# W_out's first 128 rows converted during attention; W_in's conversions at other steps

## Chip, cores, metric

The kernel runs on one core of one Trainium2 chip. The metric is the device time of one execution in microseconds (us). A profiled execution gives the rows below; its span runs from the first to the last instruction.

## What is computed

Soft-capped attention, a soft mixture of experts (MoE) on its output, and a two-matrix feed-forward block on that. W_in and W_out are float64; all else is float32. Cut from the reference:

```python
scores = cap * np.tanh(scale * np.matmul(q, k.transpose(0, 1, 3, 2)) / cap)   # 4 batches, 12 heads, 448 x 448, head_dim 64
attn = softmax(scores); x = np.matmul(attn, v)                                # -> x (1792, 768)
logits = x @ phi                                                              # 32 slots, 8 experts x 4
slot_out[e] = np.maximum(slot_input[e] @ w1[e], 0.0) @ w2[e]                  # w1 (768, 1024), w2 (1024, 768)
x = softmax(logits, 1) @ slot_out
h = x @ w_in                                                                  # w_in (768, 2048) float64
g = np.maximum(h, 0.0) + alpha * np.minimum(h, 0.0)
return (g @ w_out).astype(np.float32)                                         # w_out (2048, 768) float64
```

## The kernel before

**Attention** works on 24 pairs of heads, four steps each, one step for each chunk of 128 keys (the fourth is the tail of 64). Steps are counted by `g`, 0 to 95, and pair `i` has steps 4i to 4i+3. In a step TensorE makes the scores (`s<-qh,kh`, `s<-ql,kh`, `s<-qh,kl`: q and k are split into a high and a low part), ScalarE does tanh (L427) and exp (L428), and TensorE multiplies the result of two steps before with v (`o<-p,v`). At the second step of a pair the next pair's k and q are transposed (`tr`) and split: VectorE writes `qh`, `kl`, `ql` (L406, L384, L407). GpSimd (POOL) adds up the exponentials (`acc`, six instructions a pair), TensorE sums their rows (`rs`), VectorE collects the sums (`sums`) and after every third pair makes reciprocals (L506 to L508). At steps 20, 24, 28 and so on VectorE normalises an earlier pair's output (`xn<-xu,rb`, L532, in `norm`). ScalarE copies a pair's output from PSUM to `xu` (L453) at step 4i+5; `xu` has four buffers, so that of pair 4, written at step 21, takes the buffer of pair 0, which `xn` of pair 0 reads at step 20. PSUM has one bank for `o`, so the next pair's first `o` waits for `xu`.

**Conversion.** W_in is brought to float32 beside attention. A conversion takes 128 rows of 512 float64 words: one ScalarE instruction (L203) and four on VectorE (L204, L208, L211, L214), all in `to_f32`, all on the tile `cvbuf`. There are 24 conversions, and `cv_steps` (L743) lists the step of each. Two conversions share a buffer; two buffers take turns. Three steps after the second of two, `store_w_in` sends both results to the scratch tensor `w_in32` in DRAM and `load_w_in` behind it asks for the input of the next but one pair of conversions. Both are DMAs on SyncE's queue (SP), in the order of the program, and a DMA that waits holds the ones behind it. Engines take their instructions in a fixed order too.

**Experts.** After attention the weights of eight experts, then `w_in32` and W_out, come in through one DMA queue into slots that are used in turn. W_out arrives as float64. Its 256-row pieces are converted by `to_single` (two ScalarE and three VectorE instructions) and split by `split_wo`. The first 128 rows are treated before the last expert (L944, L945). Their load stands ahead of the last expert's weights in the queue. The feed-forward block (`mlp`) follows.

Of the kernel before, what the change touches and what calls it, by code (L numbers as in the profile page):

```python
# [8 lines left out]
F32 = mybir.dt.float32  # L9
F32R = mybir.dt.float32r  # L10
U32 = mybir.dt.uint32
AF = mybir.ActivationFunctionType
# [13 lines left out]
def tile_attention_soft_moe_mlp(ctx, tc, q, k, v, cap, phi, w1, w2, w_in, w_out, alpha, out):  # L26
    nc = tc.nc
    B, H, S, D = q.shape
    J = 4
# [3 lines left out]
    NT, DM = out.shape  # L33
    NSLOT = phi.shape[1]
    E, _, FE = w1.shape
    DFF = w_in.shape[1]
    KD = DM // 128
# [6 lines left out]
    NA = 11  # L44
# [5 lines left out]
    w_out = w_out.bitcast(U32).rearrange("f (d t) -> f d t", t=2)  # L50
# [23 lines left out]
    c_all = const.tile([P, B, J, NSLOT], F32, name="c_all")  # L74
    slotT = const.tile([128, KD, NSLOT], F32, name="slotT")
    w_in32 = dram_p.tile([DFF // 512, DM, 512], F32, name="w_in32")
    xslots = []

    def slot(i, shape, dtype=F32, name="w"):
        return arena.tile(shape, dtype, tag=f"slot{i}", name=name)  # L80
# [15 lines left out]
    where = {}  # L96
# [43 lines left out]
    def load_next(after=None):  # L140
        slot_no = may_load()
        free.remove(slot_no)
        kind, e, i = loads[nload[0]]
        nload[0] += 1
        if slot_no >= NA:

            ts = where.setdefault((kind, e, i), [])
            n = 3 if kind == "w1" else 4
            for c in range(len(ts), n):
                t = xslots[0].tile([128, SLOT // n], F32, tag=f"slot{slot_no}_{c}", name="w")  # L150
                ts.append(load_part(kind, e, i, c, t))
            return
        if kind == "w1":
            t = slot(slot_no, [128, 3, FE])
            src = w1_rows(e, i)
        elif kind == "w2":
            t = slot(slot_no, [128, 4, DM])
            src = w2_rows(e, i)
        elif kind == "wi":
            t = slot(slot_no, [128, KD, 512])  # L160
            src = w_in32[i].rearrange("(k p) f -> p k f", p=128)
        else:
            t = slot(slot_no, [128, 2, DM, 2], U32)
            src = w_out[256 * i:256 * i + 256].rearrange("(k p) f t -> p k f t", p=128)
        if kind == "w1":
            parts = [(t, src)]
        elif kind == "w2":
            parts = [(t[:, 2 * j:2 * j + 2], src[:, j]) for j in range(2)]
            if e == E - 1 and i == 1:
                parts[1:] = [(t[:, 2 + u], src[:, 1, u]) for u in range(2)]  # L170
        else:
            parts = [(t[:, c], src[:, c]) for c in range(t.shape[1])]
        if kind == "wo" and i == 0:

            half.append(parts.pop())
        elif kind == "wi" and i == 0:
            parts = [
                (t[:, ks, fs], src[:, ks, fs])
                for fs in (slice(0, 256), slice(256, 512))
                for ks in (slice(0, 3), slice(3, 6))  # L180
            ]
            parts[2:2] = half
        for dst, part in parts:
            transfer(dst, part, after)
        if kind == "w1":
            t = [t[:, c] for c in range(3)]
        elif kind == "w2":
            t = [t[:, c] for c in range(4)]
        where[kind, e, i] = t
        held[kind, e, i] = slot_no  # L190
# [63 lines left out]
    def attention():  # L254
        with ExitStack() as pools:
# [463 lines left out]

            craw, cout = {}, {}  # L720
            alpha_rows = slot(NA - 3, [KF, 128], name="alpha_rows")
            cvbuf = [slot(n, [128, 3072], U32, name="cvbuf") for n in (NA - 2, NA - 1)]

            def rows_w_in(n, of):
                fb, kk = divmod(n, KD)
                return of(fb)[kk * 128:(kk + 2) * 128].rearrange("(k p) f -> p k f", p=128)

            def load_w_in(d, after=None, halves=None):
                if 2 * d >= ncv:
                    return  # L730
                raw = cvbuf[d % 2][:, :2048].rearrange("p (k f) -> p k f", k=2)
                src = rows_w_in(2 * d, lambda fb: w_in[:, fb * 512:(fb + 1) * 512, :].rearrange("d f t -> d (f t)"))
                for ks in halves or (slice(0, 2),):
                    ins = nc.sync.dma_start(out=raw[:, ks], in_=src[:, ks])
                    if after is not None:
                        tc.add_manual_dep(ins.ins, after.ins.name, NOSYNC, reason="behind the next q")
                for k in range(2):
                    craw[2 * d + k] = raw[:, k].rearrange("p (f t) -> p f t", t=2)

            ncv = KD * (DFF // 512)  # L740


            cv_steps = [5, 7] + list(range(9, 58, J)) + [59] + list(range(61, 90, J))  # L743

            def cv_at(n):
                return cv_steps[n]

            def conv_w_in(n):
                t = cvbuf[n // 2 % 2][:, 2048:].rearrange("p (k f) -> p k f", k=2).bitcast(F32)
                to_f32(craw.pop(n), t[:, n % 2], (order[0], latest[0]))  # L750
                cout[n // 2] = t

            def store_w_in(d):
                dst = rows_w_in(2 * d, lambda fb: w_in32[fb])
                last_store[:] = [nc.sync.dma_start(out=dst, in_=cout.pop(d))]
                load_w_in(d + 2)
                if 2 * d == ncv - 2:
                    free.append(NA - 1)
# [105 lines left out]
    def tail():  # L864
# [16 lines left out]
        def rows_of(i):  # L881
            if i not in wf:
                if i in (0, 1, 2, 7):
                    wf[i] = pair({0: 0, 1: 1, 2: 2, 7: 3}[i], F32, "wf")
                else:
                    n = 2 * ((i + 1) % 2)
                    wf[i] = wx[(i - 1) // 2][:, n:n + 2]
            return wf[i]

        def to_single(i, rows=slice(0, 2)):  # L890

            raw, t = where["wo", 0, i][:, rows], rows_of(i)[:, rows]
            lo, hi, tu = raw[..., 0], raw[..., 1], t.bitcast(U32)
            v, a = nc.vector, nc.scalar
            yield "a", a.activation(out=t, in_=hi.bitcast(F32), func=AF.Abs, scale=65536.0)
            yield "v", v.tensor_scalar(out=t, in0=t, scalar1=H_MIN, scalar2=H_MAX, op0=ALU.max, op1=ALU.min)
            yield "a", a.activation(out=lo, in_=lo, func=AF.Copy, scale=LO_SCALE, bias=LO_BIAS)
            yield "v", v.scalar_tensor_tensor(
                out=tu, in0=tu, scalar=3, in1=lo, op0=ALU.logical_shift_left, op1=ALU.bitwise_or
            )  # L900
            yield "v", v.scalar_tensor_tensor(
                out=tu, in0=hi, scalar=0x80000000, in1=tu, op0=ALU.bitwise_and, op1=ALU.bitwise_or
            )
# [18 lines left out]
        def do(steps):  # L922
            for _ in steps:
                pass
# [16 lines left out]
        def experts(which, small, ps_w, yacc, warm, cstk=None):  # L941
            for e in which:
                if e == E - 1:
                    do(to_single(0, slice(0, 1)))  # L944
                    do(split_wo(0, slice(0, 1)))  # L945
                hT = small[:, 0:256].rearrange("p (u j s) -> p u j s", u=2, j=4)
                nc.gpsimd.memset(hT, 0.0)
# [492 lines left out]
        with (  # L1440
# [5 lines left out]
            with (  # L1446
# [10 lines left out]
                first = FIRST  # L1457
# [58 lines left out]
```

## Time and profile before

| | us |
|---|---|
| median of 3 runs (579.65 to 580.16) | 580.12 |
| the profiled execution | 578.89 |
| its span | 576.9 |
| attention, about | 0 to 255 |
| experts and the first loads of `mlp` | 255 to 342 |
| the rest of `mlp` | 342 to 577 |

The profiled execution is 1.2 us below the median, and 2.0 us of its own time lie outside the span. DVE is VectorE, ACT ScalarE, PE TensorE's matmuls, PEld its weight loads.

### The profile page before, as it was taken

To read this page: it belongs to the slowest core of one execution; us is meant where nothing else is said; L and a number is where in the kernel's file an instruction comes from. 1 tells how busy PE (TensorE), PEld (TensorE's weight loads), DVE (VectorE), ACT (ScalarE), POOL (GpSimd) and SP (SyncE) were. 2 spreads that over 40 slices of the span, in tenths; PEclk is the share of its full clock that TensorE was granted. 3 is DMA by queue.
4 is the path that set the end of the run, shared out by engine and by line. 5 is a ranking of instruction groups with operands and counts; after the bars stand their busy time and mean duration, and the time that the engine had idled before them with its cause. 6 is when DMAs were issued, how large, how long until landed. Compare 5 with 4: busy or idle time off the path is not lost.

```text
span 576.9 us, 11092 instructions
## 1 busy us (share of the span) xinstructions
PE 551.0 (96%) x4217; PEld 388.6 (67%) x4217; DVE 437.4 (76%) x784; ACT 387.5 (67%) x613; POOL 177.5 (31%) x158
## 2 busy tenths in 40 slices
PE   8899999999999999999996799999999999999996
PEld 5444444455444544476564667888888999999996
DVE  4799798996999679560023579998999879797974
ACT  5999999888888888530112378984777755555651
POOL 0998988685877647400000000000000000000000
PEclk9999999999999999999999999999999999999999
DMA  5876898778687875999999999200210101010101
GB/s 113 234 206 192 281 293 228 224 223 278 196 247 213 272 210 184 354 398 420 419 415 415 388 405 413 76 1 1 68 43 1 55 2 56 1 56 2 55 1 55
DMA packets 81205, 110.93 MB, mean 192 GB/s; under 512 B 52977, under 2 KB 60929, under 8 KB 79617
## 3 DMA queue, kind: packets, MB, share of 16 engines
q1 hardware_dynamic: 79376, 109.40, 56.0%
q10 hardware_dynamic: 1776, 0.84, 0.6%
q8 instruction: 33, 0.54, 0.4%
q14 instruction: 20, 0.16, 0.1%
HBM read 98.41 MB, written 11.80 MB: 191 GB/s over the span
## 4 chain that ended last, share of the span: by engine, by line
PE 65%; DVE 16%; DMA 11%; ACT 6%; issue 1%; SPq 0%; ACTq 0%; DVEq 0%
PE o L308 7%; PE P L1328 7%; PE P L1330 7%; PE P L1329 7%; PE s L308 6%; DMA w<-w_in 6%; PE oc L1102 5%; PE oc L1103 5%; PE oc L1096 5%; DMA w<-in_moe_w_dram 5%; DVE cvbuf L214 3%; PE h L952 2%; DVE cvbuf L211 2%; PE y L982 2%; ACT p L428 2%; ACT p L427 2%
## 5 line engine op out<-in xcount | busy, mean ns | idle before, releaser
L308 PE MATMUL o<-p,v 128*64 128x448 f32 (+1 forms) x384 | 93.3, 564 | 5.2 <-ACT xu L453 4.2
L428 ACT ACTIVATE p<-p,cap 128x896 f32<-128x896 f32 x96 | 91.0, 949 | 2.3
L427 ACT ACTIVATE p<-s 128x896 f32<-128x896 f32 x96 | 78.6, 820 | 18.9 <-PE s L308 15.8
L444 POOL TENSOR_TENSOR acc<-p 128x448 f32<-128x448 f32 x48 | 62.4, 1320 | 62.0 <-ACT p L428 62.0
L1102 PE MATMUL oc<-wsp,gr 128*128 128x512 f32 (+1 forms) x192 | 65.0, 339 | 0.3 <-DVE wsp L916 0.3
L1103 PE MATMUL oc<-wsp,gr 128*128 128x512 f32 (+1 forms) x192 | 64.3, 338 | 0.0
L1096 PE MATMUL oc<-wsp,gr 128*128 128x512 f32 (+1 forms) x192 | 63.6, 340 | 0.0
L308 PEld LDWEIGHTS s<-qh,kh 64*128 64x128 f32 (+1 forms) x168 | 18.0, 183 | 63.7 <-issue 24.3
L1319 ACT ACTIVATE gr<-gs 128x384 fp32r<-128x384 f32 (+1 forms) x64 | 36.8, 577 | 33.8 <-DVE gs L1303 27.8
L447 POOL TENSOR_TENSOR acc<-acc,p 64x448 f32<-64x448 f32 x46 | 57.4, 1248 | 1.7
L451 POOL TENSOR_TENSOR acc<-acc,p 128x448 f32<-128x448 f32 x46 | 54.8, 1213 | 1.7
L1320 DVE TENSOR_TENSOR gr<-gs,gr 128x384 fp32r<-128x384 f32 x64 | 39.2, 620 | 18.0 <-ACT gr L1319 18.0
L308 PE MATMUL s<-qh,kh 64*128 64x448 f32 (+1 forms) x168 | 45.3, 468 | 0.0
L1328 PE MATMUL P<-wsp,gr 128*128 128x384 f32 x128 | 42.9, 335 | 0.0
L1330 PE MATMUL P<-wsp,gr 128*128 128x384 f32 x128 | 42.8, 334 | 0.0
L1329 PE MATMUL P<-wsp,gr 128*128 128x384 f32 x128 | 42.8, 334 | 0.0
L1096 PEld LDWEIGHTS oc<-wsp,gr 128*128 128x128 f32 x192 | 36.3, 190 | 5.5 <-issue 0.6
L1102 PEld LDWEIGHTS oc<-wsp,gr 128*128 128x128 f32 x192 | 36.4, 189 | 5.3 <-DVE wsp L916 0.8
L1103 PEld LDWEIGHTS oc<-wsp,gr 128*128 128x128 f32 x192 | 36.3, 189 | 5.1 <-issue 0.8
L308 PEld LDWEIGHTS o<-p,v 128*64 128x64 f32 (+1 forms) x384 | 18.9, 134 | 28.7 <-ACT xu L453 10.9
L308 PE MATMUL s<-ql,kh 64*128 64x448 f32 (+1 forms) x168 | 35.1, 361 | 0.2 <-DVE ql L407 0.2
L308 PE MATMUL s<-qh,kl 64*128 64x448 f32 (+1 forms) x168 | 35.2, 361 | 0.0
(233 smaller groups left out, 1240.1 us busy)
## 6 DMA issues: line engine op xcount, KB each, us to landing
w<-in_moe_w_dram SPq DMA_DIRECT2D x25, 768.0 KB, 11.0
w<-in_moe_w_dram SPq DMA_DIRECT2D x12, 1536.0 KB, 10.8
w<-in_moe_w_out_dram SPq DMA_DIRECT2D x16, 768.0 KB, 10.4
cvbuf<-in_moe_w_in_dram SPq DMA_DIRECT2D x11, 1024.0 KB, 7.7
w_in<-cvbuf SPq DMA_DIRECT2D x12, 512.0 KB, 4.7
w<-in_moe_w_dram SPq DMA_DIRECT2D x12, 512.0 KB, 7.6
w<-in_moe_w_dram SPq DMA_DIRECT2D x14, 384.0 KB, 4.9
q<-in_q_dram SPq DMA_DIRECT2D x45, 112.0 KB, 3.3
```

The lines of the kernel that those rows point to most:

```text
L308: ins = nc.tensor.matmul(*a, **kw)
L427: nc.scalar.activation(out=pe, in_=ps[:, :n, :S], func=AF.Tanh)
L428: nc.scalar.activation(out=pe, in_=pe, func=AF.Exp, scale=cap_sb)
L444: nc.gpsimd.tensor_add(out=a[:, u, :], in0=pt[i, 0][:, u, :], in1=pe[:, u, :])
L447: nc.gpsimd.tensor_add(out=a[r, u, :], in0=a[r, u, :], in1=pt[i, JK][r, 0, :])
L451: nc.gpsimd.tensor_add(out=a[:, u, :], in0=a[:, u, :], in1=pe[:, u, :])
L1096: ins = nc.tensor.matmul(o, gh[:, ts], wo_h[f][:, cols], start=(f == 0 and not second), stop=False)
L1102: nc.tensor.matmul(o, gh[:, ts], wo_l[f][:, cols], start=False, stop=False)
L1103: nc.tensor.matmul(o, gl[:, ts], wo_h[f][:, cols], start=False, stop=(f == KF - 1 and not more))
L1328: nc.tensor.matmul(o, hi[:, i], bh, start=(p == 0), stop=False)
L1329: nc.tensor.matmul(o, hi[:, i], bl, start=False, stop=False)
L1330: nc.tensor.matmul(o, lo[:, i], bh, start=False, stop=(p == 7))
```

## The change

`cv_steps` gets 26 entries in place of 24. Before, they are 5, 7, 9, 13 and so on by fours to 57, then 59, then 61 to 89 by fours. After, they are 5, 7, 9, 11, 13, 15, 17, 19, then 21 to 89 by fours. So steps 11, 15 and 19 gain a conversion and step 59 loses one. The last two entries (steps 85 and 89) now convert the first 128 rows of W_out, in halves of 384 columns, and `w_out32` in DRAM takes the result. The load of these rows among the experts' weights becomes 384 KB of float32 in place of 768 KB of float64, and before the last expert one ScalarE copy replaces the five instructions of `to_single`. The two conversion buffers swap slots.

```diff
+    w_out32 = dram_p.tile([128, DM], F32, name="w_out32")
...
         if kind == "wo" and i == 0:
 
+            parts[0] = (t[:, 0].rearrange("p f t -> p (f t)")[:, :DM].bitcast(F32), w_out32)
             half.append(parts.pop())
...
-            cvbuf = [slot(n, [128, 3072], U32, name="cvbuf") for n in (NA - 2, NA - 1)]
+            cvbuf = [slot(n, [128, 3072], U32, name="cvbuf") for n in (NA - 1, NA - 2)]
...
+                if 2 * d == nwi:
+                    raw = cvbuf[d % 2][:, :2 * DM]
+                    nc.sync.dma_start(out=raw, in_=w_out[0:128].rearrange("f d t -> f (d t)"))
+                    for k in range(2):
+                        craw[nwi + k] = raw[:, k * DM:k * DM + DM].rearrange("p (f t) -> p f t", t=2)
                     return
...
-            ncv = KD * (DFF // 512)
-
-
-            cv_steps = [5, 7] + list(range(9, 58, J)) + [59] + list(range(61, 90, J))
+            nwi = KD * (DFF // 512)
+            ncv = nwi + 2
+
+
+            cv_steps = list(range(5, 20, 2)) + list(range(21, 90, J))
...
             def store_w_in(d):
-                dst = rows_w_in(2 * d, lambda fb: w_in32[fb])
+                if 2 * d == nwi:
+                    dst = w_out32.rearrange("p (k f) -> p k f", k=2)
+                else:
+                    dst = rows_w_in(2 * d, lambda fb: w_in32[fb])
...
                 if e == E - 1:
-                    do(to_single(0, slice(0, 1)))
+                    first = where["wo", 0, 0][:, 0].rearrange("p f t -> p (f t)")[:, :DM].bitcast(F32)
+                    nc.scalar.activation(out=rows_of(0)[:, 0], in_=first, func=AF.Copy)
                     do(split_wo(0, slice(0, 1)))
```

VectorE between the conversion of step 9 and the operands of pair 4 (`qh`, `kl`, `ql`), before:

```order
L214 SCALAR_TENSOR_TENSOR cvbuf<-cvbuf 128x512
L482 TENSOR_TENSOR sums<-rs,sums 128x224
L406 TENSOR_SCALAR qh<-tr,tscale 128x448
L384 TENSOR_TENSOR kl<-tr,kh 128x512
L407 SCALAR_TENSOR_TENSOR ql<-tr,tscale,qh 128x448
```

The same place after:

```order
L216 SCALAR_TENSOR_TENSOR cvbuf<-cvbuf 128x512
L484 TENSOR_TENSOR sums<-rs,sums 128x224
L206 TENSOR_SCALAR cvbuf<-cvbuf 128x512
L210 TENSOR_SCALAR cvbuf<-cvbuf 128x512
L213 SCALAR_TENSOR_TENSOR cvbuf<-cvbuf 128x512
L216 SCALAR_TENSOR_TENSOR cvbuf<-cvbuf 128x512
L408 TENSOR_SCALAR qh<-tr,tscale 128x448
L386 TENSOR_TENSOR kl<-tr,kh 128x512
L409 SCALAR_TENSOR_TENSOR ql<-tr,tscale,qh 128x448
```

The four instructions of step 11's conversion now stand ahead of pair 4's operands. Step 15's stand ahead of pair 5's in the same way.

VectorE from pair 5's `ql` to pair 6's `qh`, with the conversion of step 17 and `xn` of pair 0, before:

```order
L407 SCALAR_TENSOR_TENSOR ql<-tr,tscale,qh 128x448
L204 TENSOR_SCALAR cvbuf<-cvbuf 128x512
L208 TENSOR_SCALAR cvbuf<-cvbuf 128x512
L211 SCALAR_TENSOR_TENSOR cvbuf<-cvbuf 128x512
L214 SCALAR_TENSOR_TENSOR cvbuf<-cvbuf 128x512
L478 TENSOR_SCALAR sums<-rs,guard 128x224
L532 TENSOR_TENSOR xn<-xu,rb 128x448
L406 TENSOR_SCALAR qh<-tr,tscale 128x448
```

The same place after:

```order
L409 SCALAR_TENSOR_TENSOR ql<-tr,tscale,qh 128x448
L206 TENSOR_SCALAR cvbuf<-cvbuf 128x512
L210 TENSOR_SCALAR cvbuf<-cvbuf 128x512
L213 SCALAR_TENSOR_TENSOR cvbuf<-cvbuf 128x512
L216 SCALAR_TENSOR_TENSOR cvbuf<-cvbuf 128x512
L480 TENSOR_SCALAR sums<-rs,guard 128x224
L206 TENSOR_SCALAR cvbuf<-cvbuf 128x512
L210 TENSOR_SCALAR cvbuf<-cvbuf 128x512
L213 SCALAR_TENSOR_TENSOR cvbuf<-cvbuf 128x512
L216 SCALAR_TENSOR_TENSOR cvbuf<-cvbuf 128x512
L534 TENSOR_TENSOR xn<-xu,rb 128x448
L408 TENSOR_SCALAR qh<-tr,tscale 128x448
```

Step 19's conversion now stands ahead of `xn` of pair 0, so three added conversions (steps 11, 15, 19) precede it.

SyncE's queue from the first store (of the results of steps 5 and 7) on, before:

```order
L755 DMA w_in_72<-cvbuf 128x2x512
L734 DMA cvbuf<-in_moe_w_in_dram 128x2x1024
L359 DMA k<-in_k_dram 128x3x64 x2
L337 DMA kt<-in_k_dram 64x64 x2
L352 DMA q<-in_q_dram 112x4x64 x2
L364 DMA v<-in_v_dram 128x2x192
L340 DMA v<-in_v_dram 64x64 x2
L359 DMA k<-in_k_dram 128x3x64 x2
L337 DMA kt<-in_k_dram 64x64 x2
L352 DMA q<-in_q_dram 112x4x64 x2
L755 DMA w_in_72<-cvbuf 128x2x512
L734 DMA cvbuf<-in_moe_w_in_dram 128x2x1024
```

The same place after:

```order
L770 DMA w_in_72<-cvbuf 128x2x512
L742 DMA cvbuf<-in_moe_w_in_dram 128x2x1024
L361 DMA k<-in_k_dram 128x3x64 x2
L339 DMA kt<-in_k_dram 64x64 x2
L354 DMA q<-in_q_dram 112x4x64 x2
L366 DMA v<-in_v_dram 128x2x192
L342 DMA v<-in_v_dram 64x64 x2
L770 DMA w_in_72<-cvbuf 128x2x512
L742 DMA cvbuf<-in_moe_w_in_dram 128x2x1024
```

The first store and load keep their place; the second pair of them moves ahead of one pair's k and q.

## Rows read from the trace of the kernel before

**Rows 1.** Busy time of each engine in four stretches, columns in the first line.
```profile
core 0: us, PE busy (x) PEld busy (x) DVE busy (x) ACT busy (x) POOL busy (x), PEclk, DMA share, GB/s
19.70:36.60 16.90, 15.97 (x104) 7.47 (x106) 16.50 (x17) 16.46 (x24) 15.40 (x13) 1.00 0.81 230
36.60:53.70 17.10, 15.76 (x104) 7.31 (x100) 16.79 (x21) 16.28 (x22) 15.49 (x12) 1.00 0.73 190
141.00:143.50 2.50, 2.37 (x31) 1.28 (x34) 2.33 (x5) 2.45 (x4) 0.33 (x1) 1.00 0.96 337
255.00:342.00 87.00, 77.06 (x1126) 51.46 (x1127) 25.65 (x55) 21.64 (x40) 2.50 (x8) 1.00 1.02 411
```

**Rows 2.** Chain that ended last, us 17 to 54: start, us, what.
```profile
19.79 0.44 DVE cvbuf L204
...
53.24 0.60 PE tr L308 x4
```

**Rows 3.** VectorE in order of time: start, us, instruction; idle before in brackets.
```profile
38.01 0.67 DVE L407 SCALAR_TENSOR_TENSOR ql<-tr,tscale,qh 128x448 fp32r<-128x448 f32 x1
...
47.44 0.67 DVE L407 SCALAR_TENSOR_TENSOR ql<-tr,tscale,qh 128x448 fp32r<-128x448 f32 x1
...
53.11 0.60 DVE L532 TENSOR_TENSOR xn<-xu,rb 128x448 f32<-128x448 f32 x1
```

**Rows 4.** ScalarE in order of time, us 22 to 56.
```profile
32.95 0.92 ACT L427 ACTIVATE p<-s 128x896 f32<-128x896 f32 x1 [0.27 <-PE s L308]
...
36.31 0.69 ACT L203 ACTIVATE cvbuf<-cvbuf 128x512 f32<-128x512 f32 x1
...
54.79 0.55 ACT L453 ACTIVATE xu<-o 128x448 f32<-128x448 f32 x1 [0.38 <-PE o L308]
55.65 0.92 ACT L427 ACTIVATE p<-s 128x896 f32<-128x896 f32 x1 [0.31 <-PE s L308]
```

**Rows 5.** Tile cvbuf's instructions alone: conversions of steps 5, 7, 9, 13, 17, 57, 59.
```profile
19.70:23.90 4.20, 3.95 (x4) 0.72 (x2) 1.00 0.76 174
24.10:29.60 5.50, 5.29 (x4) 0.66 (x1) 1.00 0.76 220
31.20:36.60 5.40, 5.26 (x4) 0.29 (x1) 1.00 0.90 294
38.50:42.70 4.20, 3.93 (x4) 0.00 (x0) 1.00 0.56 114
48.00:52.90 4.90, 4.69 (x4) 0.00 (x0) 1.00 0.80 243
141.00:143.50 2.50, 2.23 (x4) 0.00 (x0) 1.00 0.96 337
144.40:150.30 5.90, 5.63 (x4) 0.71 (x2) 1.00 0.31 72
```

**Rows 6.** TensorE in order of time: the scores of steps 16 and 20 that read `ql`.
```profile
40.93 0.36 PE L308 MATMUL s<-ql,kh 64*128 64x448 f32 x2
...
49.54 0.37 PE L308 MATMUL s<-ql,kh 64*128 64x448 f32 x2
```

**Rows 7.** SyncE's load for the conversions of steps 17 and 21, and its landing.
```profile
31.52 0.41 SPq L734 DMA_DIRECT2D cvbuf<-in_moe_w_in_dram  x1
...
DMA to landing us min/median/max: 6.4/6.4/6.4
```

**Rows 8.** ScalarE at step 61: the copy of an output from PSUM.
```profile
150.84 0.55 ACT L453 ACTIVATE xu<-o 128x448 f32<-128x448 f32 x1 [0.98 <-DVE xn L532]
```

**Rows 9.** Chain that ended last, us 210 to 230.
```profile
217.08 1.39 DVE cvbuf L214
```

**Rows 10.** All engines in order of time, before the last expert's work.
```profile
310.24 0.96 DVE L916 TENSOR_TENSOR wsp<-wf,wsp 128x768 fp32r<-128x768 f32 x1 [0.96 <-ACT wsp L915]
...
312.80 1.50 PE L952 MATMUL h<-w,slotT 128*32 128x256 f32 x24 [2.10 <-DMA w<-in_moe_w_dram]
...
315.64 0.19 DVE L974 COPY small<-tp 128x32 f32<-128x32 f32 x1 [4.44 <-PE tp L969]
```

More of the change, by code (lines that the diff above doesn't have):

```diff
@@ L729, in load_w_in @@
                 if 2 * d >= ncv:
+                    return
+                if 2 * d == nwi:
[3 more added lines that the diff above has]
+                        craw[nwi + k] = raw[:, k * DM:k * DM + DM].rearrange("p (f t) -> p f t", t=2)
                     return
@@ L748, in conv_w_in @@
             def conv_w_in(n):
-                t = cvbuf[n // 2 % 2][:, 2048:].rearrange("p (k f) -> p k f", k=2).bitcast(F32)
+                t = cvbuf[n // 2 % 2][:, 2048:].bitcast(F32)
+                if n >= nwi:
+                    t = t[:, :DM]
+                t = t.rearrange("p (k f) -> p k f", k=2)
                 to_f32(craw.pop(n), t[:, n % 2], (order[0], latest[0]))
```

## The prediction

> **What bounds the kernel now.** I read the busy times by stretch first [rows 1]. In the two stretches of attention from 19.7 to 53.7 us, VectorE, ScalarE and TensorE are each busy over nine tenths of the time; VectorE has the least room, 16.50 of 16.90 and 16.79 of 17.10 us. From 255 to 342 us the DMA engines are the full ones (share 1.02 at 411 GB/s), and no other engine is. The chain that ended last comes second: it enters VectorE at 19.79 with a conversion's first instruction and leaves it at 53.24 for TensorE's transposes [rows 2]. So whatever is put on VectorE before 53.7 us is put on the path, as far as nobody had time to spare there. Third, in order of time, I looked for that time to spare, in what VectorE gives to others.
>
> - `ql` of pair 4 ends at 38.01 + 0.67 = 38.68 [rows 3], and TensorE reads it at 40.93 [rows 6]: 2.25 us to spare.
> - `ql` of pair 5 ends at 48.11 [rows 3] and is read at 49.54 [rows 6]: 1.43 us.
> - `xn` of pair 0 ends at 53.11 + 0.60 = 53.71 [rows 3], and ScalarE's `xu` of pair 4, which overwrites its input, starts at 54.79 [rows 4]: 1.08 us. The `tanh` behind it waited 0.31 us for TensorE [rows 4].
>
> **The change, part by part.**
>
> *Steps 11, 15, 19.* Three conversions come onto VectorE before `xn` of pair 0. What one costs there: the four instructions took 3.95, 5.29, 5.26, 3.93 and 4.69 us at steps 5, 7, 9, 13 and 17, 4.62 in the mean, 2.23 at step 57 and 5.63 at step 59 [rows 5]. At step 57 GpSimd was busy 0.33 of 2.50 us; in the early stretches it was busy 15.40 of 16.90 and 15.49 of 17.10 us, 0.91 [rows 1]. I take the time as growing with GpSimd's share: (4.62 - 2.23) / 0.91 = 2.6 us from none to all. The added conversions bring GpSimd no work of its own, so its share falls as the stretch gets longer.
>
> - Over the second stretch alone, 15.49 us of GpSimd in some 27.5 us is a share of 0.56, and a conversion is 2.23 + 0.56 x 2.6 = 3.7. Three are 11.1; those of steps 13 and 17 get shorter by 0.9 each; net 9.3.
> - Over both stretches, 30.9 in some 45 us is 0.69, a conversion 4.0, three 12.1, less 2 x 0.6; net 10.9.
>
> I take the middle, 10.1 us, as an estimate. Its bounds are 3 x 2.23 = 6.7 and 3 x 5.3 = 15.8. A VectorE instruction with two operands in SBUF is kept waiting by GpSimd, by the Trainium skill ("SBUF — State Buffer", section "Who interferes with whom"): the two engines have one pair of ports between them, and the loser stands until the other's whole instruction is done. The trace agrees in that the same four instructions took 2.23 us beside an idle GpSimd and up to 5.63 beside a busy one [rows 5], and by that rule alone, with 15.40 / 13 = 1.2 us for a GpSimd instruction, each of its four may wait as long as that, 4.7 us in place of the 1.5 that I add to the 2.23; three would then be some 20 us, beyond the bounds above.
>
> Where the delay appears: `ql` of pair 4 is late by one conversion of about 3.7, so TensorE stands some 1.4 us at step 16. `ql` of pair 5 comes two conversions late, at about 55, against 49.54, so some 4 us more are lost there. `xn` of pair 0 ends at 53.71 + 10.1 = 63.8, and `xu` of pair 4 starts then in place of 54.79: +9.0. The next pair's first `o` waits for `xu` with TensorE's queue behind it, and ScalarE's own queue stands behind `xu`. The 0.31 us that `tanh` waited goes: **+8.7 us**, carried on, since ScalarE and TensorE have little idle time to make it up.
>
> ScalarE's part of the three, about 0.7 us each [rows 4], I take as nothing: ScalarE now stands waiting for TensorE in the same steps, as it already did for 0.27 us at step 12 [rows 4]. Without that cover it would be 3 x 0.69 = 2.1 us.
>
> *SyncE's queue.* The second store and load go ahead of pair 5's k and q. The load for step 17's conversion in the kernel before was issued at 31.52 and landed 6.4 us later [rows 7], at 37.9. After, the same load serves step 13, whose ScalarE instruction stood at 36.31 [rows 4]: late by 1.6 us for it and for the `exp`s behind. VectorE's own delay at step 16 follows at once and swallows this, so 0; uncovered it is +1.6.
>
> *Step 59.* Its four instructions took 5.63 us [rows 5], and `xu` at step 61 waited 0.98 us for an `xn` queued behind them [rows 8]. Without them: **-0.98**, between 0 and that.
>
> *Steps 85 and 89.* Two conversions of 384 columns in place of 512, a quarter less. That of step 85 stands on the chain with one instruction of 1.39 us [rows 9]; a quarter of it and of its neighbours is some **-0.5**, between 0 and -1.
>
> *Experts.* 393,216 bytes less are read where the DMA engines are full: at 411 GB/s [rows 1] **-0.95**. The one copy in place of five instructions of `to_single` earns nothing more: `wsp` is done at 311.2, TensorE waits 2.10 us on the weights' DMA at 312.80, and the next copy on VectorE stands until 315.64 for TensorE [rows 10]. Cover gone, it would be some 2 us of VectorE and ScalarE. The swap of the two buffers changes which comes free first, and since no row prices it, I take it at 0.
>
> Sum: 8.7 - 0.98 - 0.5 - 0.95 = +6.3 on the profiled execution's 578.89: 585.2. The median is 1.23 above that execution, so **586.4 us** against 580.12.
>
> **The rivals.**
>
> 1. *The clock falls.* TensorE would stand about 4 us on pair 5's `ql`; its longest wait in these rows is 2.10 us [rows 10], and the granted clock is 1.00 in every stretch shown [rows 1]. If it falls to the 1.2 GHz level for about 4 us, TensorE, busy 15.76 of 17.10 us [rows 1], falls behind by some 3 us more: 589.5. For it: the waits are longer than any before. Against it: they may come in pieces, with the conversions between them. The Trainium skill says that an idle engine falls back to half its clock ("TensorE: Matmul & The Clock Gate", section "What's actually happening"); no row here shows that.
>
> 2. *VectorE's work is hidden, and only the load is late.* If ScalarE's wait at step 13 (1.6 us) is all that shows, 578.89 + 1.6 - 2.4 = 578.1, on the median 579.3; with a second such wait, at step 15 or 17, 580.9. About no change. Against it: VectorE's idle time before 53.7 us is 0.4 and 0.3 us in all [rows 1].
>
> 3. *Faster.* All three conversions vanish into time to spare and the three gains stand: -2.4, 577.7. It decides only if three conversions delay `xu` of pair 4 by less than 2.4 us, that is 1.08 of slack, 0.31 and 2.4 together, 3.8 us in all or 1.3 each. No conversion in [rows 5] is under 2.23, so other work would have to shrink by three fifths of each, as it would if GpSimd's adds, no longer pressed, let VectorE's other instructions through much faster.
>
> **How the numbers follow.** The forecast gets 0.65, the clock 0.15, rival 2 0.07, rival 3 0.08; 0.05 is left for slower in other ways. With the lower bound of the conversions, 6.7 us, `xu` is late by 5.6, and the sum is 5.3 - 2.4 = +2.9: 583.0 on the median's basis. With the upper, 15.8, it is late by 14.7, the sum is +12.0: 592.1, which takes in the clock's 589.5 as well. The range is 582.5 to 592. What this kernel's runs can tell from no change is 0.2%, 1.2 us. Rival 3 is faster by more than that, rival 2 lies within it for the most part, the rest is slower: 0.08, 0.07, 0.85.
>
> **What would show it.** Right: the chain that ended last stays on VectorE to the `xn` of pair 0, which ends near 64; TensorE waits for `ql` at steps 16 and 20; `xu` of pair 4 starts near 64; later steps keep their lengths, step 61 gets shorter by a microsecond, and the stretch from the experts' start to 342 loses one. Wrong: `xn` of pair 0 ends before 58, or `xu` waits for the `o` before it and not for `xn`; ScalarE waits for a DMA longer than for TensorE; TensorE's granted clock falls below 1.00 between 40 and 65 us; or steps after 22 make up what was lost, for instance because GpSimd has caught up and no longer holds VectorE.

## The result, and the profile after

The changed kernel takes **586.19 us** in the median of 6 runs (584.25 to 588.72), the kernel before 579.88 (6 runs, 578.98 to 580.49): the ratio is **1.0112, with a 95% interval of 1.0082 to 1.0143**. Forecast were 586.4 us, in a range of 582.5 to 592.

The profiled execution took 587.68 us with a span of 585.9, so it is one of the longer ones, 9.0 us above the span before. I read it by the starts of the `tanh` of each step (L429 after, L427 before):

| start of | before | after | later by |
|---|---|---|---|
| step 0 | 8.76 | 9.27 | 0.5 |
| step 22 | 55.65 | 63.98 | 8.3 |
| step 42 | 99.92 | 109.45 | 9.5 |
| step 44 | 105.18 | 118.43 | 13.3 |
| step 62 | 151.28 | 163.70 | 12.4 |
| step 89 | 221.48 | 233.59 | 12.1 |
| step 91 | 228.10 | 238.91 | 10.8 |
| step 95 | 238.94 | 249.76 | 10.8 |
| end of the span | 576.9 | 585.9 | 9.0 |

So 7.8 us are lost from step 0 to 22, where the three conversions were added, and 3.7 at steps 42 and 43, of which the forecast knew nothing; from step 22 to 42 another 1.2 goes in small pieces, and the rest are gains.

The chain that ended last, after (start, us, what), stays on VectorE, through the conversion of step 11 at 37.40, until `ql` of pair 5 ends at 55.4. From there to `xu` of pair 4 at 63.53 the view follows TensorE (the pieces left out in the second gap are all its own), which ran at half clock for much of that time. It answers to [rows 2]:

```profile
37.40 1.00 DVE cvbuf L206
38.42 1.26 DVE cvbuf L210
39.70 0.70 DVE cvbuf L213
40.42 0.69 DVE cvbuf L216
...
54.69 0.68 DVE ql L409
55.41 1.11 PE s L310 x4
...
62.71 0.82 PE s L310 x4
63.53 0.55 ACT xu L455
```

VectorE in order of time shows `xn` of pair 0, which answers to the last row of [rows 3]. It ends at 63.44, and `xu` starts 0.09 us behind it, as it does behind each `xn` that it waits for in e1, e4 and e6; so `xu` waited for VectorE, although the view puts its wait down to the scores that ended just before. e4, where TensorE is kept at full clock, shows the same order without that doubt.

```profile
62.83 0.61 DVE L534 TENSOR_TENSOR xn<-xu,rb 128x448 f32<-128x448 f32 x1
```

Tile `cvbuf` alone, as in [rows 5], for the conversions of steps 11, 13, 15, 17 and 19 after:

```profile
core 0: us, DVE busy (x) ACT busy (x), PEclk, DMA share, GB/s
37.30:41.15 3.85, 3.69 (x4) 0.67 (x1) 0.99 0.68 137
42.80:48.35 5.55, 5.43 (x4) 0.19 (x1) 0.85 1.04 297
50.15:53.60 3.45, 2.98 (x4) 0.65 (x1) 1.00 0.16 46
55.25:60.30 5.05, 4.92 (x4) 0.00 (x0) 0.50 0.96 276
60.55:62.95 2.40, 2.22 (x4) 0.00 (x0) 0.79 0.63 118
```

The three added ones took 3.69 + 2.98 + 2.22 = 8.9 us of VectorE, and those of steps 13 and 17 got longer, not shorter, by 5.43 - 3.93 = 1.5 and 4.92 - 4.69 = 0.2. Together that is 10.6, where the forecast had 10.1.

The busy times by stretch, as in [rows 1], with one stretch more: VectorE has no more room than before, and the others are the ones that wait.

```profile
19.70:36.60 16.90, 15.47 (x100) 7.19 (x100) 16.17 (x17) 16.77 (x25) 15.22 (x12) 1.00 0.80 231
36.60:53.70 17.10, 13.99 (x83) 5.67 (x81) 16.82 (x22) 14.13 (x20) 12.36 (x10) 0.90 0.68 177
53.70:66.00 12.30, 10.44 (x47) 5.55 (x51) 11.81 (x18) 6.47 (x10) 5.89 (x5) 0.72 0.76 200
```

ScalarE falls from 16.28 [rows 1] to 14.13 us in the second stretch, GpSimd from 15.49 to 12.36 and then to 5.89 of 12.30, a share of 0.48: the conversion of step 19, at 2.22 us, met no GpSimd any more. GpSimd stood still because ScalarE's exponentials came late:

```profile
41.48 2.23 POOL L446 TENSOR_TENSOR acc<-p 128x448 f32<-128x448 f32 x2 [2.10 <-ACT p L430]
```

And the granted clock is no longer 1.00.

ScalarE and, in the second fence, TensorE in order of time show where the waits are (idle time before in brackets):

```profile
38.42 0.67 ACT L205 ACTIVATE cvbuf<-cvbuf 128x512 f32<-128x512 f32 x1 [1.40 <-DVE cvbuf L206]
...
45.20 0.92 ACT L429 ACTIVATE p<-s 128x896 f32<-128x896 f32 x1 [1.28 <-PE s L310]
...
56.62 0.92 ACT L429 ACTIVATE p<-s 128x896 f32<-128x896 f32 x1 [2.58 <-PE s L310]
...
60.37 0.55 ACT L429 ACTIVATE p<-s 128x448 f32<-128x448 f32 x1 [1.75 <-PE s L310]
```

```profile
39.57 0.97 PE L310 MATMUL o<-p,v 128*64 128x448 f32 x4 [1.86 <-ACT xu L455]
...
54.31 0.47 PE L310 MATMUL s<-qh,kh 64*128 64x448 f32 x2 [1.86 <-DVE qh L408]
...
55.41 0.74 PE L310 MATMUL s<-ql,kh 64*128 64x448 f32 x2 [0.63 <-DVE ql L409]
...
111.59 0.97 PE L310 MATMUL o<-p,v 128*64 128x448 f32 x4 [2.25 <-DMA v<-in_v_dram]
```

The first of the ACT rows is put down to a VectorE instruction that had long been done. In its place it is the load: issued at 31.45, it landed 6.87 us later, at 38.32. The wait for `ql` of pair 4 at step 16 that I forecast does not show; that step was late already, by this load. In e7, whose load landed in time, it does: 1.30 us for `qh` and 0.63 for `ql`. Behind each of the other waits TensorE's clock fell. Short stretches, columns as above:

```profile
40.00:44.00 4.00, 4.00 (x22) 0.98 (x18) 3.97 (x6) 3.78 (x5) 2.52 (x3) 0.63 0.56 149
...
52.00:54.00 2.00, 0.45 (x4) 0.00 (x0) 1.97 (x3) 2.00 (x3) 2.00 (x2) 1.00 0.00 0
...
56.00:58.00 2.00, 2.00 (x10) 0.80 (x6) 1.97 (x2) 1.34 (x2) 1.92 (x2) 0.50 0.83 175
...
114.00:116.00 2.00, 2.00 (x20) 0.63 (x16) 0.00 (x0) 1.79 (x2) 1.93 (x3) 0.50 1.04 205
```

0.50 is the 1.2 GHz level. TensorE was busy 0.45 of 2.00 us from 52 to 54 and ran at half clock from 56 to 60; it waited 2.25 us at 109 to 111.6 and ran at half clock from 114 to 116.

### The profile page after: what moved, and what is told of

The parts are those of the page before. It is cut to its first block, busy times and chain, and to the rows that moved or that the text cites. A ratio compares the mean times of both kernels' runs of the same rounds, so it can differ in the third digit from the quotient of the medians.

```text
span 585.9 us, 11106 instructions
## 1 busy us (share of the span) xinstructions
PE 557.7 (95%) x4217; PEld 391.9 (67%) x4217; DVE 431.4 (74%) x789; ACT 387.3 (66%) x614; POOL 173.1 (30%) x158
## 4 chain that ended last, share of the span: by engine, by line
PE 70%; DVE 13%; DMA 9%; ACT 6%; issue 2%; SPq 0%; ACTq 0%; DVEq 0%
PE o L310 8%; PE s L310 7%; PE P L1346 7%; PE P L1344 7%; PE P L1345 7%; PE oc L1118 5%; PE oc L1119 5%; PE oc L1112 5%; DMA w<-w_in 5%; PE h L968 3%; PE y L998 3%; DVE cvbuf L216 2%; DVE cvbuf L213 2%; ACT p L430 2%; PE nx L310 2%; PE tr L310 2%
## 5 line engine op out<-in xcount | busy, mean ns | idle before, releaser
L310 PE MATMUL o<-p,v 128*64 128x448 f32 (+1 forms) x384 | 94.8, 572 | 8.3 <-ACT xu L455 5.7
L429 ACT ACTIVATE p<-s 128x896 f32<-128x896 f32 x96 | 78.6, 820 | 27.0 <-PE s L310 23.9
L446 POOL TENSOR_TENSOR acc<-p 128x448 f32<-128x448 f32 x48 | 60.2, 1274 | 77.2 <-ACT p L430 77.2
L449 POOL TENSOR_TENSOR acc<-acc,p 64x448 f32<-64x448 f32 x46 | 55.1, 1199 | 1.7
```

Of the source, the lines that this page charges most:

```text
L310: ins = nc.tensor.matmul(*a, **kw)
L429: nc.scalar.activation(out=pe, in_=ps[:, :n, :S], func=AF.Tanh)
L446: nc.gpsimd.tensor_add(out=a[:, u, :], in0=pt[i, 0][:, u, :], in1=pe[:, u, :])
L449: nc.gpsimd.tensor_add(out=a[r, u, :], in0=a[r, u, :], in1=pt[i, JK][r, 0, :])
```

## The experiments

The theory at the outset: the added VectorE work ahead of `xn` of pair 0 is the loss, its size is set by how busy GpSimd is beside it, and W_out's part gives a little back. The rivals: W_out's part costs the time; the queue does; the clock does; a conversion costs the same wherever it stands. All in medians, with the kernel before run on the same chip beside them (`list` is `cv_steps`):

| kernel | us (lowest to highest) | kernel before | ratio, 95% interval |
|---|---|---|---|
| e1 early steps alone | 589.33 (588.28 to 590.58) | 579.57 | 1.0152 to 1.0188 |
| e2 W_out late | 584.81 (583.35 to 586.52) | 579.57 | 1.0062 to 1.0096 |
| e3 stores later | 585.21 (584.80 to 585.44) | 579.57 | 1.0082 to 1.0111 |
| e4 TensorE filled | 585.40 (582.69 to 587.27) | 579.57 | 1.0073 to 1.0119 |
| e5 steps 23 and 35 | 579.51 (577.61 to 583.25) | 579.48 | 0.9988 to 1.0017 |
| e6 steps 19 and 35 | 582.91 (581.19 to 584.78) | 579.48 | 1.0046 to 1.0084 |
| e7 steps 11 and 35 | 583.29 (581.83 to 584.88) | 579.48 | 1.0051 to 1.0081 |
| e8 less GpSimd work | 578.87 (576.66 to 581.09) | 579.48 | 0.9970 to 1.0003 |
| e9 steps 24, 36, 60 | 584.38 (583.77 to 584.89) | 579.20 | 1.0077 to 1.0103 |
| e10 steps 20 and 35 | 581.52 (579.39 to 584.50) | 579.20 | 1.0025 to 1.0054 |
| e11 W_out's part, no conversion | 585.40 (584.65 to 585.56) | 579.20 | 1.0093 to 1.0119 |
| e12 the same, buffers as before | 581.41 (580.29 to 584.36) | 578.98 | 1.0032 to 1.0060 |

### Which half of the change costs: e1, e2

```diff
-            cv_steps = [5, 7] + list(range(9, 58, J)) + [59] + list(range(61, 90, J))
+            cv_steps = list(range(5, 20, 2)) + list(range(21, 82, J))
```

> The kernel before with the early list of steps alone: W_in's 24 conversions at steps 5 to 19 by twos and 21 to 81 by fours, W_out untouched. Theory (the early steps cost the time, W_out's part gives some back): 10 to 11 us of added VectorE work before xn of pair 0 as in the changed kernel, so the step of xu of pair 4 starts 7 to 8 us late; step 59's 0.98 is gained, steps 85 and 89 have no conversion and gain 1 to 2, the experts gain nothing: 584 to 587 us. Rival (W_out's store, load and copy cost the time): near 579.

Step 22 started at 63.58, with step 0 at 8.79: 7.9 us lost between the two, as in the changed kernel (7.8), without anything of W_out. That half of the theory stands. The end was 2 to 5 us beyond what was expected: from the start of step 95 to the end of the span this kernel took 341.3 us, the kernel before 338.0, and the DMA engines were at a share of 0.13 from 230 to 235 us and 0.60 from 235 to 240. Which load held the queue there I did not settle.

```diff
-            cv_steps = list(range(5, 20, 2)) + list(range(21, 90, J))
+            cv_steps = [5, 7] + list(range(9, 54, J)) + [55, 57] + list(range(61, 78, J)) + [79, 81, 83, 85, 89]
```

> The changed kernel with its W_out part, but no conversion moved early: steps 5, 7, 9 to 53 by fours, 55, 57, 61 to 77 by fours, 79, 81, 83, 85, 89. Theory: VectorE has idle time at steps 55, 56 and 79 to 84 (1.10 of 3.42, 1.30 of 2.44, 1.16 of 3.42 us busy), so two more conversions there cost less than 1 us, step 59's 0.98 and the experts' 0.95 are gained: 577.5 to 579.5 us, faster than before. Rival (two more conversions cost 3.5 us each wherever they stand): 584 or more.

A miss, and the time is the rival's, though not in the rival's way, by which a conversion costs the same wherever it stands. Up to step 79 the kernel stood 0.3 us ahead of the kernel before; then steps 80 and 81 took 5.6 us more and steps 85 and 86 another 4.9. The new conversion of step 79 stands on VectorE ahead of an `xnat` that TensorE's queue waits for, and the clock falls behind that wait. TensorE in order of time, and two stretches:

```profile
200.26 0.77 PE L310 MATMUL rb<-rh,sel 128*128 128x224 f32 x2 [2.85 <-DVE xnat L557]
```

```profile
196.00:200.00 4.00, 1.41 (x12) 0.93 (x10) 3.80 (x4) 2.06 (x3) 3.85 (x4) 1.00 1.01 259
200.00:205.00 5.00, 4.74 (x15) 2.92 (x16) 2.73 (x5) 0.55 (x1) 0.59 (x1) 0.51 0.61 197
```

A step whose VectorE is half idle on the average may still have its instructions placed so that four more of them stand ahead of the one that is waited for.

### The queue and the clock: e3, e4

```diff
-                        if n % 2 and cv_at(n) == g - (2 if n == ncv - 1 else 3):
+                        if n % 2 and cv_at(n) == g - (2 if n == ncv - 1 else 7 if 25 <= cv_at(n) < 80 else 3):
```

> The changed kernel with the stores and loads from step 28 to 80 four steps later, which puts the v of a pair ahead of them in SyncE's queue, as in the kernel before. In the profile of the changed kernel TensorE waited 2.25 us for v at step 42 and ran at a granted clock of 0.50 to 0.69 for the next 4 us; steps 42 and 43 took 3.7 us more than before. Theory (the order in the queue makes that wait, in some executions): the wait and the low clock at steps 42 and 43 are gone, and the time is 583 to 585 us with less spread than the changed kernel's 584.3 to 588.7. Rival (the wait is chance, or comes from the full DMA engines): 586, with the same spread.

As the theory had it, with a median 0.2 us above its range: steps 42 and 43 took 1.90 and 3.36 us, as before the change, no matmul of TensorE waited for a DMA from 66 us to the end of attention, the clock was 1.00 there, and the 4 runs lie within 0.64 us of each other, the changed kernel's 6 within 4.5. So the 3.7 us of the changed kernel's profile go with the order in SyncE's queue. There, the load for the conversions went ahead of a pair's v (start, us):

```profile
102.24 0.41 SPq L742 DMA_DIRECT2D cvbuf<-in_moe_w_in_dram  x1
102.75 0.86 SPq L366 DMA_DIRECT2D v<-in_v_dram  x1
103.65 2.19 SPq L342 DMA_DIRECT2D v<-in_v_dram  x2
```

and v landed 7.6 to 8.7 us after its issue, at a time when the DMA engines were full (0.95 to 1.02 from 108 to 114 us). The order makes the wait possible and no more: e1 and e8 have it too and waited 2.17 and 1.36 us for v there, and so has e4, where v, issued at 99.91, landed at 107.14, in time, and steps 42 and 43 took no longer than before the change. That fits the spread of the changed kernel's runs, 584.25 to 588.72, and a median that fell by only 1.0 us, which the intervals don't tell from nothing.

```diff
+                if now[0] == 20:
+                    for _ in range(15):
+                        matmul(ps[:, 0, :128], ident, ident, start=True, stop=True)
...
+                if g == 14:
+                    t = ps_s.tile([128, 2, 512], F32, tag="s", name="s")
+                    for _ in range(13):
+                        matmul(t[:, 0, :128], ident, ident, start=True, stop=True)
+                    spare_s.append(t)
```

> The changed kernel with small matmuls of the identity on TensorE where it waited (13 before the first o of pair 3, 15 before the scores of step 20); they write a bank that is overwritten, and change no result. Theory (the waits lower the granted clock, and this costs 2 to 3 us over steps 15 and 20 to 21): the granted clock stays near 1.00 from 38 to 62 us and the time falls by 1.5 to 3 us against the changed kernel, 583 to 585. Rival (VectorE sets the pace there, the clock only fills its waits): clock up, time within 0.7 us of the changed kernel's 586.2.

The clock stayed at 1.00 in all stretches that I read from 38 to 46 and from 52 to 62 us, for instance

```profile
54.00:56.00 2.00, 2.00 (x19) 1.86 (x20) 1.97 (x3) 0.00 (x0) 1.93 (x2) 1.00 0.98 239
56.00:58.00 2.00, 2.00 (x13) 0.87 (x10) 1.93 (x3) 1.41 (x2) 1.92 (x3) 1.00 0.99 388
```

and step 22 started 54.25 us after step 0, where it was 54.71 in the changed kernel: 0.5 us. By the median it is 0.8 less, with spreads that overlap. The rival is nearer: VectorE sets the pace, and most of the low clock lies in its shadow, for `xu` of pair 4 still waits for `xn`:

```profile
62.72 0.54 ACT L460 ACTIVATE xu<-o 128x448 f32<-128x448 f32 x1 [1.24 <-DVE xn L539]
```

By step 28 this kernel was 0.9 us ahead of the changed one, so some of the clock's price comes behind the wait. That an idle TensorE falls back to half its clock, as the Trainium skill says ("TensorE: Matmul & The Clock Gate", section "What's actually happening"), the traces show at 56 and 114 us; here it is worth 1 us or less, where I had given 3.

These kernels also price the late load of step 13. ScalarE waited for it 0.25 us in e3, 0.61 in e4, 1.40 in the changed kernel and 2.18 in e1, and all four had lost 7.4 to 8.0 us by step 22, the most with the shortest wait. While VectorE is full, the load is covered.

### The price of one early conversion: e5, e6, e7

All three have the kernel before's list, 59 included, with step 35 and one more added, and W_out's part.

```diff
-            cv_steps = list(range(5, 20, 2)) + list(range(21, 90, J))
+            cv_steps = [5, 7, 9, 13, 17, 21, 23, 25, 29, 33, 35, 37, 41, 45, 49, 53, 57, 59, 61, 65, 69, 73, 77, 81, 85, 89]
```

(e5; e6 has 19 and e7 has 11 in place of 23.)

> The changed kernel with W_out's part as it is, and the list of the kernel before with steps 23 and 35 added (26 entries, 59 kept, none of 11, 15, 19). Theory (what a conversion costs is VectorE's idle time at its step: VectorE was busy 1.15 of 2.02, 0.62 of 2.05 and 1.93 of 2.59 us in steps 23 to 25 and the same in 35 to 37): both fit there for less than 1 us in all, steps 85 and 89 give back 0.5 to 1.3, the experts 1 to 1.8: 577 to 579 us, faster than before. Rival (two more conversions cost 2 us or more each wherever they stand, by VectorE, GpSimd or the queue): 583 or more.

> As the kernel with steps 23 and 35 added, but with 19 in place of 23: one early conversion, right ahead of xn of pair 0. Theory: it took 2.2 us there in the changed kernel, xn of pair 0 had 1.08 us to spare and the tanh behind it 0.31, so step 22 starts 0.8 to 1.5 us later than without it. Rival (the three early conversions only hurt together): within 0.5 us of the kernel with 23.

> As the kernel with steps 23 and 35 added, but with 11 in place of 23: one early conversion, ahead of pair 4's operands. Theory: 3.7 us on VectorE, with 1.43 us to spare at ql of pair 5 and 1.39 at xn of pair 0: step 22 starts 2 to 2.5 us late. Rival (a third of the three's 7.8 us): 2.6 us; rival (the later load for step 13 alone): 1.6 us at step 13 and no more behind.

e5 came out even with the kernel before, within 0.2%, where 577 to 579 us were expected: the two conversions cost 2.2 us by the start of step 42 (93.4 us after step 0, before 91.2) in place of less than 1, and steps 89 and 90 together gave back 1.3, the stretch behind step 95 0.6. Its steps 25 and 37 took 3.37 us against 2.59, since `xn` stood behind the conversion, on ScalarE:

```profile
65.04 0.54 ACT L455 ACTIVATE xu<-o 128x448 f32<-128x448 f32 x1 [0.81 <-DVE xn L534]
```

e6 and e7 missed upward: step 22 came 3.15 us late with step 19 alone and 4.9 with step 11 alone. The conversion of step 19 now took this (tile `cvbuf` alone), and `xu` waited for it:

```profile
53.35:57.90 4.55, 4.42 (x4) 0.68 (x1) 1.00 0.23 51
```

```profile
58.55 0.54 ACT L455 ACTIVATE xu<-o 128x448 f32<-128x448 f32 x1 [3.88 <-DVE xn L534]
```

4.42 us in place of 2.22: in the changed kernel two conversions stood ahead of it and had left GpSimd without work. The delay is still 4.4 + 0.1 less the 1.08 + 0.31 to spare.

In e7 nothing was to spare. The conversion of step 11 took 4.51 us, those of steps 13 and 17 4.92 and 5.04, 1.3 more together than before, and one instruction behind a reciprocal (L510) 0.45 in place of 1.31 (L508). `xn` of pair 0 ended 4.88 us late, and step 22 was as late. `xu` ran 1.08 us behind that `xn`, as in the kernel before: not by spare time, but because both hang on VectorE's `sums`, the instruction ahead of `xn`. TensorE's transposes of the next q wait for `sums`, and `o` and `xu` come behind them. TensorE, before and in e7:

```profile
53.24 0.60 PE L308 MATMUL tr<-ident,q 112*128 112x112 f32 x4 [0.59 <-DVE sums L478]
```

```profile
58.30 0.60 PE L310 MATMUL tr<-ident,q 112*128 112x112 f32 x4 [1.71 <-DVE sums L480]
```

So the 1.08 us are there for work between `sums` and `xn`, as step 19's is, and not for work ahead of `sums`, as that of steps 11 and 15. One early conversion costs 3.2 to 4.9, three of them 7.8. An added one took 4.4 to 4.5 us alone and 3.7, 3.0 and 2.2 as one of three, where GpSimd had less to do; that part the forecast had assumed.

### GpSimd beside VectorE: e8

```diff
-                        if i < NPAIR - 1:
+                        if i < NPAIR - 1 and not 2 <= i <= 5:
                             nc.gpsimd.tensor_add(out=a[r, u, :], in0=a[r, u, :], in1=pt[i, JK][r, 0, :])
...
-                    if i < NPAIR - 1:
+                    if i < NPAIR - 1 and not 2 <= i <= 5:
                         for u in range(2):
                             nc.gpsimd.tensor_add(out=a[:, u, :], in0=a[:, u, :], in1=pe[:, u, :])
```

> The changed kernel without GpSimd's second and third add (the tail's and that of the chunk behind it) for pairs 2 to 5, so that the sums of these pairs leave out two of their four chunks. Theory (the time of a conversion grows with GpSimd's busy time): with about a third of GpSimd's work the conversions of steps 11 to 19 take 2.3 to 3.3 us each in place of 3.7, 5.5, 3.0, 4.9 and 2.2, and xn of pair 0 ends 4 to 7 us earlier than in the changed kernel, 580 to 583 us in all. Rival (they take the time of their own, GpSimd only shows beside them): no change, 586.

The largest effect of all: 578.87 us, 7.3 less than the changed kernel and below the 580 to 583 expected, with every early conversion still there. The five conversions of steps 11 to 19 took

```profile
35.20:37.55 2.35, 2.23 (x4) 0.00 (x0) 1.00 1.01 350
39.90:42.30 2.40, 2.24 (x4) 0.01 (x1) 0.50 0.57 186
46.40:49.05 2.65, 2.16 (x4) 0.00 (x0) 1.00 0.82 173
51.50:53.90 2.40, 2.24 (x4) 0.00 (x0) 1.00 0.67 211
54.75:57.95 3.20, 3.05 (x4) 0.00 (x0) 1.00 0.94 318
```

11.9 us in place of 19.2, and `xn` of pair 0 ended 4.5 us earlier, counted from step 0. VectorE then had idle time (13.27 of 17.10 us busy), and what bound the stretch was the load of step 13: ScalarE waited 2.77 us for it, which is the second rival's mechanism, seen once VectorE no longer covers it:

```profile
39.26 0.66 ACT L205 ACTIVATE cvbuf<-cvbuf 128x512 f32<-128x512 f32 x1 [2.77 <-DMA cvbuf<-in_moe_w_in_dram]
```

Step 16 came 5.4 us late, counted from step 0, step 22 only 4.2. In the profiles this kernel was 3.7 us ahead of the changed one at step 22 and 7.0 at step 44, since its steps 42 and 43 took 6.5 us in place of 9.0. Those 2.5 us go with the wait for v at step 42, which was shorter here, so what GpSimd's adds are shown to cost by way of VectorE is 3.7 of the 7.8 us, with the load's wait in place of the rest.

### Ahead of xn or behind it: e9, e10

```diff
-            cv_steps = [5, 7, 9, 13, 17, 21, 23, 25, 29, 33, 35, 37, 41, 45, 49, 53, 57, 59, 61, 65, 69, 73, 77, 81, 85, 89]
+            cv_steps = [5, 7, 9, 13, 17, 21, 24, 25, 29, 33, 36, 37, 41, 45, 49, 53, 57, 60, 61, 65, 69, 73, 77, 81, 85, 89]
```

(e9, against e5; e10 is e6 with 20 in place of 19.)

> The kernel with steps 23 and 35 added, with its conversions of steps 23, 35 and 59 one step later (24, 36, 60), which on VectorE puts each behind the xn of its step in place of ahead of it, and moves nothing else there. In that kernel's profile steps 25 and 37 took 0.78 us more than in the kernel before, since xu waited 0.81 us for an xn behind the conversion, and step 61 still had its 0.98. Theory (a conversion costs what it delays an xn that an xu waits for): 0.8 at steps 25 and 37 and 0.98 at 61 go, ScalarE's 0.5 at an even step comes instead: 577 to 578.5 us, faster than before. Rival (VectorE's time counts wherever it stands): no change against the kernel with 23 and 35, 579.5.

> The kernel with one early conversion at step 19, with that conversion at step 20: on VectorE its four instructions stand behind xn of pair 0 in place of ahead of it, and nothing else moves. At step 19 xu of pair 4 waited 3.88 us for xn and step 22 started 3.15 us late. Theory (the wait of xu for xn is the price): step 22 starts within 0.7 us of the kernel before; pair 6's ql, 3.2 us to spare, is late by about 1.3 at step 24; in all 1.5 to 2.5 us less than with step 19, 580.5 to 581.5 us. Rival (4.5 us of VectorE are lost wherever they stand in a full stretch): same as with 19, 582.9.

e10 did nearly what was expected of it: step 22 started within 0.1 us of the kernel before, counted from step 0, and the median is 1.4 below e6's, where 1.5 to 2.5 were expected. But step 25 then took 4.15 us in place of 2.59, and of the 3.0 us that it was ahead of e6 at step 22, 1.0 was left at step 26. e9 shows the same more strongly and missed by 6 us and more, and its rival (no change) by 5: steps 25, 37 and 61 did lose their wait (2.44, 2.43 and 2.44 us), but steps 27, 29, 31 and 33 took 0.3 to 0.7 more each, and step 65 4.49 in place of 2.59, for the next `xn` behind conversions:

```profile
167.78 0.54 ACT L455 ACTIVATE xu<-o 128x448 f32<-128x448 f32 x1 [1.90 <-DVE xn L534]
```

At step 41 another 4.0 went. There the conversions of steps 36 and 37 stood ahead of a `sums`, TensorE waited for that, and the clock was at 0.50 from 104 to 106 us; `xu` waited 2.96 us for TensorE:

```profile
103.16 0.60 PE L310 MATMUL tr<-ident,q 112*128 112x112 f32 x4 [2.58 <-DVE sums L484]
```

So `xn` and `xu` are where the loss shows first, not what it is: in a full stretch VectorE's time is lost at the next instruction that somebody waits for. My narrower theory, that the wait of `xu` is the price, falls.

### W_out's part by itself: e11, e12

```diff
-            cv_steps = list(range(5, 20, 2)) + list(range(21, 90, J))
+            cv_steps = [5, 7] + list(range(9, 58, J)) + [59] + list(range(61, 90, J))
...
-            ncv = nwi + 2
+            ncv = nwi
...
+                if 2 * d == nwi - 2:
+                    last_store[:] = [nc.sync.dma_start(out=w_out32.rearrange("p (k f) -> p k f", k=2), in_=cvbuf[d % 2][:, 2048:].bitcast(F32)[:, :DM].rearrange("p (k f) -> p k f", k=2))]
```

> The changed kernel's W_out part alone: the 24 steps of the kernel before, W_out's first 128 rows loaded as 384 KB of float32 and copied once, but their conversion left out (the scratch tensor gets some of W_in's results in their place, so the output's share of these 128 rows is wrong). Theory: attention as before but for the end, the experts' stretch shorter by the 0.95 us of 393,216 bytes, and 85 and 89 as before: 578.3 to 579.2 us. Rival (the five instructions of to_single stood on the path too): 577 to 578.

```diff
-            cvbuf = [slot(n, [128, 3072], U32, name="cvbuf") for n in (NA - 1, NA - 2)]
+            cvbuf = [slot(n, [128, 3072], U32, name="cvbuf") for n in (NA - 2, NA - 1)]
```

> The kernel with W_out's part alone and its conversion left out, with the two conversion buffers back in the slots of the kernel before (24 conversions end in the other buffer than 26, and the buffer of the last one is the slot that is given to the experts' weights first; with the slots swapped that kernel lost 5.9 us behind attention, with the DMA engines at a share of 0.18 from 225 to 230 us against 0.67 before). Theory (the swap was the loss, W_out's part itself gains the 0.95 us of its bytes): the stretch behind attention is 0.5 to 1.5 us shorter than the kernel before's 338.0, 578.0 to 579.0 us. Rival (the added store or the load of float32 costs the time): 583 or more, as with the swap.

Both missed. They had attention as before (step 95 at 230.3 us after step 0, before 230.2) and lost behind it: 343.9 us from step 95 to the end in e11 and 339.6 in e12, against 338.0. In e11 the DMA engines stood idle most of the time here:

```profile
225.00:230.00 5.00, 4.16 (x44) 2.23 (x46) 4.93 (x9) 3.65 (x6) 2.20 (x2) 1.00 0.18 46
```

The swap of the buffers, undone, gave back 4.0 us in the median. As I read it, the swap keeps the buffer of the last conversion in the slot that is given up last, which 26 conversions need and 24 do not. The remaining 1.6 us of e12 are a flaw of the experiment as far as I can see: its added store stands last in place of W_in's, and two loads of weights that SyncE issued at 225.71 in the kernel before came at 230.36. W_out's gain was not isolated, then. What speaks for it is the stretch from step 95 to the end in the ten profiled kernels with 26 conversions (the changed one and e2 to e10): 336.1 to 337.4, 337.0 in the mean, against 338.0 in the one profile of before.

## Why the prediction was right, point by point

- **VectorE's chain.** Right, and nearly in size: 10.6 us of added time in conversions against 10.1. `ql` of pair 5 ended at 55.4 ("about 55"), `xn` of pair 0 at 63.4 (63.8), `xu` of pair 4 started at 63.5 (63.8). Counted from step 0, which started 0.5 later than before, `xn` was 9.2 late; L510 behind the reciprocal took 0.44 us where L508 had taken 1.31. That makes +7.8 us by step 22, forecast +8.7. e1, e3 and e4 lose 7.4 to 8.0 us by step 22 whatever the queue and the clock do there, and e8 shows GpSimd's part in the price.
- **The 1.08 us to spare at `xn`.** Read as if it held for all of VectorE's delay. It holds only for work between `sums` and `xn` (e7). In the sum it came out the same, since step 19's conversion stands there and is longer than 1.08.
- **The conversions of steps 13 and 17 getting shorter.** Wrong: they took 5.43 and 4.92 us. GpSimd's share fell at the end of the stretch, to 0.48, and not evenly over it. The two errors, 8.9 for three added ones (forecast 11.1 to 12.1) and +1.7 for the old ones (forecast -1.2 to -1.8), cancel.
- **The bound by the port rule.** By the Trainium skill ("SBUF — State Buffer", section "Who interferes with whom") a loser waits for the whole instruction of the other engine; I had put that at up to 1.2 us an instruction and 20 us in all. The trace agrees with the rule in kind: one and the same instruction takes one of two times, 0.69 or 1.51 us. The size is 0.82 us, and three conversions took 8.9.
- **The load of step 13.** Priced at 1.6 us and covered: 1.40 in the profile, and step 13 was 1.5 longer. It was covered by step 22, since waits of 0.25 to 2.18 us went with the same loss there; in e8, where VectorE has time, it decides.
- **Step 59: -0.98.** Step 61 took 2.59 us in place of 3.56: right.
- **Steps 85 and 89: -0.5.** Too small, and in another place: in the changed kernel steps 85 to 88 took as long as before and steps 89 and 90 1.3 less, as in e3 to e10 (1.6 in e2, and in e1, which has no conversion there); with the full ones they took no less (e11, e12).
- **Experts: -0.95.** -1.8 in this profile, -1.0 in the mean of ten; right as far as it was measured. The swap at 0 is not contradicted for the change as made, which was not run without it; with 24 conversions the same swap costs 4 us (e11 against e12).
- **Not forecast.** v behind the load at step 42, 3.7 us with the clock behind it in the profiled execution. The medians have it in part, and e3, which removes it, is 1.0 below the changed kernel; so 586.2 would be about 585.2 without it, against a forecast of 586.4. The 1.2 us from step 22 to 42 were not forecast either; later steps were to keep their lengths. The near hit of the median is partly luck.
- **The signs.** `xn` ended near 64 and `xu` followed it at once. But the chain left VectorE at 55.4 for TensorE, TensorE did not wait for `ql` at step 16, and the granted clock fell to 0.50, which was named as a sign of being wrong; by e4 it did not decide the time.
- **The rivals.** The clock did fall, at 40, 56 and 114 us, and was worth 1 us or less before step 28 (e4). The hidden-VectorE and the faster cases did not come near: e6 shows 3.2 us lost for one conversion, where they needed less than 1.3.

No kernel that computes the reference beat the kernel before: e5, the best, is even with it.

## What to carry to other kernels

Ahead of moving work to an engine that stands at 98% busy, look in order of time for the next results that others wait for: the delay of each, less its time to spare, is the price, and moving the work behind one of them only hands the delay on to the next. Time to spare at one result is none if another result ahead of it, here `sums`, leads to the same wait. Price an instruction on VectorE by what GpSimd does beside it; less GpSimd work there was worth 3.7 of the 7.8 us by step 22. And when the parity of a schedule changes, look at what it does to the queue: a load of 1 MB that changes places with a small one that is needed at once cost 3.7 us in one profile, some 50 us behind the last added step.

## What the runs showed of the hardware

One VectorE instruction of a conversion takes one of two times: beside a busy GpSimd in the changed kernel, and with little of it in e8 (VectorE in order of time):

```profile
45.31 1.51 DVE L213 SCALAR_TENSOR_TENSOR cvbuf<-cvbuf 128x512 uint32<-128x512 uint32 x1
46.86 1.52 DVE L216 SCALAR_TENSOR_TENSOR cvbuf<-cvbuf 128x512 uint32<-128x512 uint32 x1
```

```profile
40.87 0.69 DVE L213 SCALAR_TENSOR_TENSOR cvbuf<-cvbuf 128x512 uint32<-128x512 uint32 x1
41.59 0.69 DVE L216 SCALAR_TENSOR_TENSOR cvbuf<-cvbuf 128x512 uint32<-128x512 uint32 x1
```

The difference is 0.82 us each time, the same on `L210` (0.43 and 1.25), so a conversion of four costs 2.2 to some 5.5 us. I had expected times spread between the two. Only the first of the four, `L206`, has them: 0.36 to 1.41 us over the changed kernel's conversions of 512 columns.
